# Sums of the last 64 keys as four products of 144 queries for both heads, the two partial sums joined one pair later, and v in one transfer

## The chip, the cores and the metric

The kernel runs on one core of a Trainium2 chip. The metric is the device time of one execution in microseconds; before the change the median of three runs is 551.17 us (551.02 to 552.08). Five engines work side by side, each through its own instructions in order: TensorE (PE, matmuls; its weight loads have a row of their own, PEld), VectorE (DVE), ScalarE (ACT), GpSimd (POOL) and SyncE (SP, which here only issues DMA transfers).

## The reference

Three stages in float32: attention over 4 batches of 8 heads, then a gated layer with a spatial product, then a second gated layer with a short convolution. The change lies in the first.

```python
q_rot, k_rot = (rotate(q), rotate(k))                       # 4 x 8 heads, 576 positions, 64 wide
scores = scale * np.matmul(q_rot, k_rot.transpose(0, 1, 3, 2))
scores = scores - np.max(scores, axis=-1, keepdims=True)
attn = np.exp(scores)
attn = attn / (np.sum(attn, axis=-1, keepdims=True) + 1e-09)
return np.matmul(attn, v)
...
h = gelu(x @ w_in); u, v = halves(h); v_n = layernorm(v) * g_ln
x = x + (u * (w_sg @ v_n + b_sg)) @ w_out                   # then conv gate, w_val, w_out2
```

## The kernel before

Two heads are worked on together: there are 16 **pairs** i = 0 to 15. For a pair, the scores are made transposed (keys on the partitions, 576 queries in two halves of 288) in nine **units**: eight of 128 keys and one half of the queries for both heads (line 663), and a ninth with the last 64 keys of both heads stacked on the 128 partitions (line 671). ACT turns each unit into exponentials, tiles `e0` to `e8` (line 676).

The queries' maxima are found one pair ahead. During the **phase** of pair i (its nine units), TensorE also makes seven score products of pair i+1 with queries on the partitions (line 611 six times, line 621 last), and VectorE reduces them to maxima (lines 614, 629, 623). All these products go through four PSUM slots of two banks. In a phase the slots are used round robin, 0 1 2 3: the first product is one of line 611 in slot 0, and the fifth, a unit of scores, takes slot 0 again, so it needs the first maximum to have been read. The slots come from a small greedy model in the code (`free`, `pe`, `ac`, `dv`).

After its phase a pair is finished: 64 instructions of exponentials by v (line 700; one float32 product is two instructions, and four products run side by side on the four groups of 32 columns of the array), then the **sums** of the exponentials (`sum_unit`, line 735): groups of four products with weights of ones, over pairs of tiles, over the POOL's running sums `ac`, and over `e8`; then the last 64 keys by v (line 710). ACT and DVE copy the result out (`xu`, line 715 on DVE). The sums go by ACT to `ss`, by a DMA to `rc`, and a pair later through a reciprocal (line 747) and a DMA to `r_d` (`sum_end`).

VectorE's work from one phase to the next, here called a **turn**, is in this order: last maximum of pair i+1 (line 623), rotation of pair i+2 (four instructions of line 260), then for pairs 1 to 8 a quarter of a weight's conversion (lines 310 to 316), for pairs 9 to 14 a low part `kl` (line 260), the reciprocal of pair i-1 somewhere among these, the copy `xu` of pair i, and then the first maximum of the next phase. A POOL instruction on one element, `mark` (line 268), holds back the POOL until VectorE has passed its two-input work.

The order on every engine is made by a planner (`Plan.order`): each task has a cost in us, and the planner simulates the engines with these costs; TensorE's order is fixed as written, that of the others follows due times. A changed cost or task can so move others. From about 234 us on the two later stages run (line 843 for most of their products).

Of the kernel before, what the change touches and what calls it, by code (L numbers as in the profile page):

```python
# [170 lines left out]
def mixer_kernel(ctx: ExitStack, tc: tile.TileContext, qk, v, vrem, cs, w_in, g_ln, w_sgT, b_sg,  # L171
# [63 lines left out]
    VM = tiles(att, "vm", 2, [128, 4, 2, 64], F32)  # L235
    VR = tiles(att, "vr", 2, [128, 64], F32)
# [4 lines left out]
    RC = tiles(att, "rc", 2, [128, 9], F32)  # L241
# [5 lines left out]
    ones = att.tile([128, 32], F32, name="ones")  # L247
    ones_b = [att.tile([128, 32], F32, name=f"ones_b{h}") for h in range(2)]
# [27 lines left out]
    def setup():  # L276
# [3 lines left out]
        def consts():  # L280
            nc.gpsimd.memset(one_r.bitcast(F32), 0.0)
            nc.gpsimd.memset(one_b.bitcast(F32), 0.0)
            for h in range(2):
                nc.gpsimd.memset(ones_b[h], 0.0)
            nc.gpsimd.memset(ones, 1.0)
            nc.gpsimd.memset(mhalf, -0.5)
            for t in (*XS, *RB):
                nc.gpsimd.memset(t[:, 0:4], 0.0)
            for h in range(2):
                nc.gpsimd.memset(one_r[64 * h:64 * h + 1, :].bitcast(F32), 1.0)  # L290
                nc.gpsimd.memset(one_b[64 * h:64 * h + 1, 64 * h:64 * h + 64].bitcast(F32), 1.0)
                nc.gpsimd.memset(ones_b[h][64 * h:64 * h + 64], 1.0)
# [355 lines left out]
    ne = [0]  # L648
    EU = {}

    def st_unit(i, u, ps, kps):
# [38 lines left out]
    def pv_unit(i, us):  # L690
# [3 lines left out]
        if us[0] < 8:  # L694
            j = UNITS[us[0]][0]

            def mm():
                for h in range(2):
                    for t in range(4):
                        nc.tensor.matmul(pv[32 * t:32 * t + 32, h, 0:HALF], VM[j2][:, j, h, 32 * (t % 2):32 * (t % 2) + 32],  # L700
# [5 lines left out]
        def mm():  # L706
            for hf in range(2):
                for h in range(2):
                    rows = slice(64 * h, 64 * h + 64)
                    nc.tensor.matmul(pv[64 * hf:64 * hf + 64, h, 0:HALF], VR[j2][rows], e[rows, hf], start=False, stop=True,  # L710
                                     skip_group_check=True)
        add("PE", FP32 + 0.1, mm, [("e", EU[i, 8]), ("vr", j2)], [kp])
# [10 lines left out]
    def sum_unit(i, ps, kps):  # L723

        j2 = i % 2
        src = [(ones, ones, [(E[EU[i, u + hf]], h) for h in range(2) for hf in range(2)], ("e", EU[i, u]),
                ("e", EU[i, u + 1])) for u in (4, 6)[adds(i) // 2 - 1:]]
        src.append((ones, ones, [(AC[hf], h) for h in range(2) for hf in range(2)], ("ac", 0), ("ac", 1)))
# [10 lines left out]
        add("Act", act(HALF), lambda: nc.scalar.activation(ss, ps[:, 0, 0:HALF], AF.Copy, bias=1e-9), [kps], [("ss", 0)])  # L739
# [26 lines left out]
    def attention():  # L766
# [3 lines left out]
        def phase(i, vl):  # L770

            order = "ytyttxtttyttyxTS" if i + 1 < NPAIR else "ttttttttT"
            if not i:
                order = "xtttyttytyttyxTS"
            free = [0.0, 0.0, 0.74 if i else 0.0, 0.0]
            pe, ac, dv = 0.2, 0.0, 0.0
            nt, xs, ys = 0, iter(range(2)), iter(range(2, 6))
            for x, what in enumerate(order):
                ks = range(4) if x < len(order) - 4 else range(3)
                at_once = [k for k in ks if free[k] <= pe]  # L780
                k = max(at_once, key=lambda k: free[k]) if at_once else min(ks, key=lambda k: free[k])
                pe = max(pe, free[k])
                if what in "tT":
                    pe += 4 * PASS if what == "t" else 8 * PASS + 0.24
                    act_at = max(ac, pe + 0.22)
                    ac, free[k] = act_at + 0.55, act_at + 0.75
                    st_unit(i, nt, PS[k], ("ps", k))
                    add_unit(i, nt)
                    nt += 1
# [454 lines left out]
```

## Time and profile before

| | |
|---|---|
| median of 3 runs | 551.17 us (551.02 to 552.08) |
| the profiled execution: its own time | 550.86 us |
| the profiled execution: span, first to last instruction | 549.1 us |
| mean granted TensorE clock | 0.999 |
| busy PE, PEld | 541.2 us, 462.5 us |
| busy DVE, ACT, POOL | 416.6 us, 278.4 us, 245.7 us |
| chain that ended last | PE 97%, DVE 1% |
| line 735 (sums), per instruction | 406 ns, 464 instructions |

The profile's times are microseconds from the span's start. An instruction's duration includes the way through the engine's pipeline, so the next one may start before it ends; what an instruction costs its engine is the step from its start to the next start. Idle time in brackets is that of the engine ahead of the instruction, with what ended it.

### The profile page before, as it was taken

To read this page: it belongs to the slowest core of one execution; us is meant where nothing else is said; L and a number is where in the kernel's file an instruction comes from. 1 tells how busy PE (TensorE), PEld (TensorE's weight loads), DVE (VectorE), ACT (ScalarE), POOL (GpSimd) and SP (SyncE) were. 2 spreads that over 40 slices of the span, in tenths; PEclk is the share of its full clock that TensorE was granted. 3 is DMA by queue.
4 is the path that set the end of the run, shared out by engine and by line. 5 is a ranking of instruction groups with operands and counts; after the bars stand their busy time and mean duration, and the time that the engine had idled before them with its cause. 6 is when DMAs were issued, how large, how long until landed. Compare 5 with 4: busy or idle time off the path is not lost.

```text
span 549.1 us, 12848 instructions
## 1 busy us (share of the span) xinstructions
PE 541.2 (99%) x5104; PEld 462.5 (84%) x5104; DVE 416.6 (76%) x611; ACT 278.4 (51%) x451; POOL 245.7 (45%) x229
## 2 busy tenths in 40 slices
PE   7999999999999999999999999999999999999996
PEld 6877777777777777679989989989999998899985
DVE  7878888888888888878478845663989997659610
ACT  3566767667766667635527136135156443333221
POOL 6545555555555555446886776653610011222000
PEclk9999999999999999999999999999999999999999
DMA  5565656565556673773384752634264212110022
GB/s 193 136 186 154 194 143 189 150 178 175 168 164 161 185 205 95 216 240 93 133 280 134 223 198 74 210 113 144 106 214 130 66 45 78 38 58 1 0 78 96
DMA packets 58028, 77.46 MB, mean 141 GB/s; under 512 B 29392, under 2 KB 34000, under 8 KB 57968
## 3 DMA queue, kind: packets, MB, share of 16 engines
q1 hardware_dynamic: 57664, 76.37, 45.8%
q8 instruction: 40, 0.66, 0.5%
q10 hardware_dynamic: 304, 0.26, 0.1%
q14 instruction: 20, 0.16, 0.1%
HBM read 55.94 MB, written 18.95 MB: 136 GB/s over the span
## 4 chain that ended last, share of the span: by engine, by line
PE 97%; DVE 1%; POOL 0%; ACT 0%; issue 0%; ACTq 0%; POOLq 0%
PE psa L843 55%; PE psa L663 13%; PE psa L700 12%; PE psa L735 5%; PE psa L611 4%; PE psa L671 4%; PE psa L710 2%; PE psa L954 2%; PE psa L756 1%; DVE mx L614 1%; PE psa L621 1%; DVE raw L260 0%; DVE mn L623 0%; POOL mr L295 0%; ACT ob L264 0%
## 5 line engine op out<-in xcount | busy, mean ns | idle before, releaser
L614 DVE TENSOR_REDUCE mx<-psa 128x2 f32<-128x640 f32 (+1 forms) x96 | 88.7, 954 | 21.9 <-PE psa L611 14.6
L676 ACT ACTIVATE e<-psa 128x576 f32<-128x576 f32 x144 | 88.1, 652 | 20.9 <-PE psa L671 10.3
L700 PE MATMUL psa<-e,vm 128*32 128x288 f32 x1024 | 65.4, 408 | 0.0
L700 PEld LDWEIGHTS psa<-e,vm 128*32 128x32 f32 x1024 | 31.6, 110 | 27.8 <-issue 2.6
L261 POOL TENSOR_TENSOR ac<-e,e 128x576 f32<-128x576 f32 x32 | 45.0, 1425 | 8.2 <-ACT e L676 8.2
L843 PE MATMUL psa<-s_h,vn 128*128 128x288 f32 x256 | 46.9, 295 | 0.0
L260 DVE TENSOR_TENSOR raw<-raw,cst 128x1152 f32<-128x1152 f32 (+1 forms) x33 | 41.9, 1271 | 0.3 <-DMA raw<-qk 0.3
L264 ACT CAST qp<-raw 128x512 fp32r<-128x512 f32 x16 | 19.1, 1192 | 43.6 <-DVE raw L260 43.6
L663 PE MATMUL psa<-qh,kh 64*128 64x288 f32 x256 | 39.6, 305 | 0.0
L843 PEld LDWEIGHTS psa<-s_h,vn 128*128 128x128 f32 x256 | 38.3, 188 | 0.0
L663 PE MATMUL psa<-qh,kl 64*128 64x288 f32 x256 | 37.9, 292 | 0.0
L663 PE MATMUL psa<-ql,kh 64*128 64x288 f32 x256 | 37.9, 292 | 0.0
L663 PE MATMUL psa<-mr,one_r 64*128 64x288 f32 x256 | 37.7, 290 | 0.0
L261 POOL TENSOR_TENSOR vs<-vs,u 128x576 f32<-128x576 f32 x16 | 26.7, 1666 | 20.7 <-DVE vs L958 20.7
L611 PE MATMUL psa<-kh,qp 64*128 64x320 f32 (+1 forms) x256 | 32.8, 312 | 0.7 <-ACT kh L264 0.7
L1035 DVE SCALAR_TENSOR_TENSOR gt<-xm,cw,gt 128x576 f32<-128x576 f32 x32 | 28.9, 909 | 1.8 <-ACT gt L1032 1.4
L611 PEld LDWEIGHTS psa<-kh,qp 64*128 64x128 f32 x256 | 21.6, 184 | 8.0 <-ACT ss L739 3.9
L843 PE MATMUL psa<-XL,w_h 128*128 128x288 f32 x128 | 27.4, 296 | 0.0
L843 PE MATMUL psa<-XH,w_h 128*128 128x288 f32 x128 | 27.4, 295 | 0.0
L843 PE MATMUL psa<-XH,w_l 128*128 128x288 f32 x128 | 27.4, 295 | 0.0
L843 PE MATMUL psa<-s_l,vn 128*128 128x288 f32 x128 | 27.2, 294 | 0.0
L261 POOL TENSOR_TENSOR xl<-xs,xh 128x576 fp32r<-128x576 f32 x2 | 4.6, 2322 | 48.8 <-ACT xh L264 48.8
(182 smaller groups left out, 1488.2 us busy)
## 6 DMA issues: line engine op xcount, KB each, us to landing
raw<-qk SPq DMA_DIRECT2D x31, 576.0 KB
xu_d<-xu SPq DMA_DIRECT2D x32, 144.0 KB
rb<-r_d SPq DMA_DIRECT2D x32, 144.0 KB
xs<-xu_d SPq DMA_DIRECT2D x16, 288.0 KB
x_d<-xs SPq DMA_DIRECT2D x16, 288.0 KB
g_d<-vs SPq DMA_DIRECT2D x16, 288.0 KB
vm<-v SPq DMA_DIRECT2D x16, 256.0 KB
wr<-w_in SPq DMA_DIRECT2D x8, 512.0 KB
```

Of the source, the lines that this page charges most:

```text
L260: return add("DVE", dve(n), lambda: nc.vector.tensor_tensor(out_(), a(), b(), op), r, w, after, lock=True)
L261: return add("Pool", pool(n), lambda: nc.gpsimd.tensor_tensor(out_(), a(), b(), op), r, w, after, lock=True)
L264: return add("Act", act(n), lambda: nc.scalar.copy(out_(), in_()), r, w, after)
L611: nc.tensor.matmul(ps[:, h, w * y:w * y + w], QP[j2][rows, c], kh[rows, keys], start=True, stop=True)
L614: add("DVE", MAXIMA[n // 2 > 0][1], lambda: nc.vector.tensor_reduce(out=MX[j2][:, n // 2 > 0, :, chunks[0]:chunks[-1] + 1], in_=ps[:, :, 0 ...
L663: nc.tensor.matmul(ps[:, h, 0:HALF], x[rows, keys] if o < 3 else x[rows], y[rows, cols], start=o == 0, stop=o == 3)
L671: nc.tensor.matmul(ps[:, hf, 0:HALF], x, y[:, cols], start=o == 0, stop=o == 3)
L676: add("Act", 0.62, lambda: nc.scalar.activation(E[n], ps[:, :, 0:HALF], AF.Exp), [kps], [("e", n)])
L700: nc.tensor.matmul(pv[32 * t:32 * t + 32, h, 0:HALF], VM[j2][:, j, h, 32 * (t % 2):32 * (t % 2) + 32], E[EU[i, us[t // 2]]][:, h], start=j ...
L735: nc.tensor.matmul(ps[32 * t:32 * t + 32, 0, 0:HALF], x[t // 2], a[:, y], start=n == 0, stop=n == len(src) - 1, skip_group_check=True)
L843: nc.tensor.matmul(out_(y), lhs(p, k, y), rhs(q, k, y), start=not z, stop=ends and z == len(terms) - 1)
L1035: add("DVE", dve(S) + 0.05, lambda dd=dd, m=m, x2=x2, gt=gt: nc.vector.scalar_tensor_tensor(gt(), x2()[:, m:m + S], cw[:, 5 * dd + m:5 * d ...
```

## The change

- `sum_unit`: the products of `e8` with ones covered 288 queries of one head each (two weights `ones_b`, one for each head's 64 partitions). Now each covers 144 queries and both heads: the weight `ones_b` has ones for head h in columns 16h to 16h+15, and the four products, on the four column groups, take two halves of 288 in two slices of 144. So that a column group can hold both heads, the other sums use two weights `ones0`, `ones1`, with ones in 16 of the 32 columns and zeros in the others. The number of instructions is the same; eight of them per pair are half as long.
- The total of a query then lies in two rows of PSUM. Two DMAs instead of one bring both parts to `rc` (now 128 x 3 x 9), and in `sum_end` a `tensor_reduce` on VectorE adds them ahead of the reciprocal; two DMAs instead of one bring the result to `r_d`.
- `v` and its last 64 keys come in one DMA per pair instead of two.
- Two more memsets in the setup, for the new weights.
- The slots of a phase are written out (`ORDERS`) instead of computed; the numbers are the same as the greedy model gave. The numbers of the `e` tiles are also the same.
- The planner's cost of the sums falls by half a float32 product, and it gets the new tasks.

```diff
+ORDERS = ('xtttyttytyttyxTS', '0123012301230120'), ('ytyttxtttyttyxTS', '0123012301230120'), ('ttttttttT', '012012012')
...
-    RC = tiles(att, "rc", 2, [128, 9], F32)
+    RC = tiles(att, "rc", 2, [128, 3, 9], F32)
...
+            nc.gpsimd.memset(ones_b, 0.0)
             for h in range(2):
-                nc.gpsimd.memset(ones_b[h], 0.0)
-            nc.gpsimd.memset(ones, 1.0)
+                nc.gpsimd.memset(ones[h], 0.0)
+                nc.gpsimd.memset(ones[h][:, 16 * h:16 * h + 16], 1.0)
...
-        def ld(q):
-            q.dma_start(out=VM[j2].rearrange("p c h d -> p (c h d)"), in_=v[i // HP, i % HP])
-            q.dma_start(out=VR[j2], in_=vrem[i // HP, i % HP])
-        dma(290, ld, w=[("vm", j2), ("vr", j2)], after=after, n=2)
+        dma(290, lambda q: q.dma_start(out=VM[j2], in_=v[i // HP, i % HP]), w=[("vm", j2)], after=after)
...
-        src.append((*ones_b, [(E[e], hf) for h in range(2) for hf in range(2)], ("e", e)))
 
         def mm():
             for n, x in enumerate(src):
-                for t, (a, y) in enumerate(x[2]):
-                    nc.tensor.matmul(ps[32 * t:32 * t + 32, 0, 0:HALF], x[t // 2], a[:, y], start=n == 0,
-                                     stop=n == len(src) - 1, skip_group_check=True)
-        add("PE", len(src) * FP32, mm, [*[k for x in src for k in x[3:]], ("consts",)], [kps])
+                for t, (a, h) in enumerate(x[0]):
+                    nc.tensor.matmul(ps[32 * t:32 * t + 32, 0, 0:HALF], ones[h], a[:, h], start=n == 0, stop=False, skip_group_check=True)
+            for t in range(4):
+                cc = slice(144 * (t // 2), 144 * (t // 2) + 144)
+                nc.tensor.matmul(ps[32 * t:32 * t + 32, 0, cc], ones_b, E[e][:, t % 2, cc], start=False, stop=True, skip_group_check=True)
+        add("PE", (len(src) + 0.5) * FP32, mm, [*[k for x in src for k in x[1:]], ("e", e), ("consts",)], [kps])
...
         def rows(q):
-            q.dma_start(out=rc, in_=ss[0:97:32].rearrange("t (p c) -> t p c", c=9))
-        dma(5, rows, [("ss", 0)], [("rc", j2)])
+            for y in range(2):
+                q.dma_start(out=rc[:, y], in_=ss[64 * y:64 * y + 49:16].rearrange("t (p c) -> t p c", c=9))
+        dma(5, rows, [("ss", 0)], [("rc", j2)], n=2)
...
-        add("DVE", 0.25, lambda: nc.vector.reciprocal(rc, rc), w=[("rc", i % 2)], after=after)
-        dma(5, lambda q: q.dma_start(out=r_d[i // HP][i % HP].rearrange("(p c) -> p c", c=9), in_=rc), [("rc", i % 2)], [("r_d", i)])
+        add("DVE", 0.15, lambda: nc.vector.tensor_reduce(out=rc[:, 2], in_=rc[:, 0:2].rearrange("p y c -> p c y"), axis=AX.X, op=ALU.add),
+            w=[("rc", i % 2)], after=after)
+        add("DVE", 0.25, lambda: nc.vector.reciprocal(rc[:, 2], rc[:, 2]), w=[("rc", i % 2)], after=after)
```

How this moves VectorE's work. First the turn after an odd pair (here i = 1), from the last quarter of a conversion (`wf`) to the first maximum (`mx`); `xu` is the copy out of PSUM. Before:

```order
42 L316 SCALAR_TENSOR_TENSOR wf_120<-wr_119,wt_121 128x256
43 L747 RECIPROCAL rc_172<-rc_172 128x9
44 L715 COPY xu_170<-psa 128x288
45 L614 TENSOR_REDUCE mx_151<-psa 128x2 x2
46 L614 TENSOR_REDUCE mx_151<-psa 128x2x2
```

And now:

```order
42 L317 SCALAR_TENSOR_TENSOR wf_120<-wr_119,wt_121 128x256
43 L744 TENSOR_REDUCE rc_170<-rc_170 128x9
44 L746 RECIPROCAL rc_170<-rc_170 128x9
45 L710 COPY xu_168<-psa 128x288
46 L612 TENSOR_REDUCE mx_151<-psa 128x2 x2
```

The joining stands directly ahead of the reciprocal that reads its result, and both ahead of the copy and the maximum. The same holds after pairs 3, 5 and 7, and, behind `kl` instead of `wf`, after pairs 9 to 13.

Then the turn after an even pair (here i = 2), from the last maximum (`mn`, from PSUM) to the copy. Before:

```order
50 L623 TENSOR_REDUCE mn_153<-psa 128x1
51 L747 RECIPROCAL rc_173<-rc_173 128x9
52 L260 TENSOR_TENSOR raw_123<-raw_123,cst 128x1152
53 L260 TENSOR_TENSOR raw_123<-raw_123 128x576
54 L260 TENSOR_TENSOR raw_123<-raw_123,cst 128x1152
55 L260 TENSOR_TENSOR raw_123<-raw_123 128x576
56 L310 TENSOR_SCALAR wt_121<-wt_121 128x256
57 L312 TENSOR_SCALAR wt_121<-wt_121 128x256
58 L314 SCALAR_TENSOR_TENSOR wt_121<-wr_119,wt_121 128x256
59 L316 SCALAR_TENSOR_TENSOR wf_120<-wr_119,wt_121 128x256
60 L715 COPY xu_169<-psa 128x288
```

And now:

```order
51 L621 TENSOR_REDUCE mn_153<-psa 128x1
52 L744 TENSOR_REDUCE rc_171<-rc_171 128x9
53 L260 TENSOR_TENSOR raw_123<-raw_123,cst 128x1152
54 L260 TENSOR_TENSOR raw_123<-raw_123 128x576
55 L260 TENSOR_TENSOR raw_123<-raw_123,cst 128x1152
56 L260 TENSOR_TENSOR raw_123<-raw_123 128x576
57 L311 TENSOR_SCALAR wt_121<-wt_121 128x256
58 L313 TENSOR_SCALAR wt_121<-wt_121 128x256
59 L315 SCALAR_TENSOR_TENSOR wt_121<-wr_119,wt_121 128x256
60 L317 SCALAR_TENSOR_TENSOR wf_120<-wr_119,wt_121 128x256
61 L746 RECIPROCAL rc_171<-rc_171 128x9
```

The joining has taken the reciprocal's place, and the reciprocal stands behind the conversion, just ahead of the copy. The same holds after pairs 4, 6 and 8.

On the POOL, at the program's start, the memsets ahead of those that TensorE waits for. Before, from the first to the one after the weights:

```order
8 L284 MEMSET ones_b_180 128x32
9 L284 MEMSET ones_b_181 128x32
10 L285 MEMSET ones 128x32
11 L286 MEMSET mhalf 128x1
12 L288 MEMSET xs_107 128x4
```

And now:

```order
8 L283 MEMSET ones_b 128x32
9 L285 MEMSET ones_177 128x32
10 L286 MEMSET ones_177 128x16
11 L285 MEMSET ones_178 128x32
12 L286 MEMSET ones_178 128x16
13 L287 MEMSET mhalf 128x1
```

Two memsets are new, and each of the two of 16 columns writes over part of the one just ahead of it.

## Rows read from the trace of the kernel before

**Rows 1.** The page: busy time of the engines, and the chain by engine.
```profile
PE 541.2 (99%) x5104; PEld 462.5 (84%) x5104; DVE 416.6 (76%) x611; ACT 278.4 (51%) x451; POOL 245.7 (45%) x229
...
PE 97%; DVE 1%; POOL 0%; ACT 0%; issue 0%; ACTq 0%; POOLq 0%
```

**Rows 2.** TensorE in order of time, end of pair 3: start, duration, engine, instruction.
```profile
72.06 0.43 PE L735 MATMUL psa<-ac,ones 128*32 128x288 f32 x4
...
72.30 0.67 PE L735 MATMUL psa<-e,ones_b 128*32 128x288 f32 x8
72.90 0.71 PE L710 MATMUL psa<-e,vr 64*64 64x288 f32 x8
73.55 0.41 PE L611 MATMUL psa<-kh,qp 64*128 64x320 f32 x2
```

**Rows 3.** TensorE's weight loads at the fifth product of the next phase.
```profile
74.74 0.19 PEld L663 LDWEIGHTS psa<-mr,one_r 64*128 64x128 f32 x2
74.99 0.19 PEld L663 LDWEIGHTS psa<-qh,kh 64*128 64x128 f32 x2
```

**Rows 4.** VectorE in order of time, the turn after pair 3.
```profile
67.36 0.17 DVE L629 TENSOR_REDUCE mn<-mx 128x8 fp32r<-128x16 f32 x1
67.45 0.75 DVE L623 TENSOR_REDUCE mn<-psa 128x1 fp32r<-128x576 f32 x1
68.12 1.35 DVE L260 TENSOR_TENSOR raw<-raw,cst 128x1152 f32<-128x1152 f32 x1
69.50 0.76 DVE L260 TENSOR_TENSOR raw<-raw 128x576 f32<-128x576 f32 x1
...
73.34 0.42 DVE L316 SCALAR_TENSOR_TENSOR wf<-wr,wt 128x256 int32<-128x256 int32 x1
73.69 0.21 DVE L747 RECIPROCAL rc<-rc 128x9 f32<-128x9 f32 x1
73.81 0.40 DVE L715 COPY xu<-psa 128x288 f32<-128x288 f32 x1
74.12 0.81 DVE L614 TENSOR_REDUCE mx<-psa 128x2 f32<-128x640 f32 x1
```

**Rows 5.** VectorE, the copy after pair 0, then the turn after pair 9.
```profile
32.40 0.46 DVE L715 COPY xu<-psa 128x288 f32<-128x288 f32 x1 [1.47 <-PE psa L710]
...
155.64 0.20 DVE L747 RECIPROCAL rc<-rc 128x9 f32<-128x9 f32 x1
156.02 0.46 DVE L715 COPY xu<-psa 128x288 f32<-128x288 f32 x1 [0.17 <-issue]
```

**Rows 6.** The start: POOL, TensorE and VectorE in order of time.
```profile
1.57 0.12 POOL L292 MEMSET ones_b<- 64x32 f32 x1
1.73 0.20 POOL L290 MEMSET one_r<- 1x128 f32 x1
...
2.77 6.50 PE L756 MATMUL psa<-mr,one_r 128*128 128x512 f32 x16 [2.77 <-POOL mr L295]
...
9.74 3.82 DVE L614 TENSOR_REDUCE mx<-psa 128x4 f32<-128x1024 f32 x4 [0.21 <-PE psa L611]
```

**Rows 7.** From attention to the next stage: VectorE, TensorE, POOL, TensorE.
```profile
232.54 1.58 DVE L260 TENSOR_TENSOR XL<-xs,XH 128x576 fp32r<-128x576 f32 x2
...
234.81 0.73 PE L843 MATMUL psa<-w_h,XH 128*128 128x512 f32 x2
...
249.62 1.30 POOL L261 TENSOR_TENSOR w_l<-wf,w_h 128x512 fp32r<-128x512 f32 x1 [5.25 <-ACT w_h L264]
...
251.47 0.42 PE L843 MATMUL psa<-XH,w_l 128*128 128x288 f32 x2
```

**Rows 8.** VectorE beside the POOL: all of line 629 (min/median/max ns), and single instructions.
```profile
L629 DVE TENSOR_REDUCE mn<-mx x16: 170/170/173, 15.7 to 216.7; 128x8 fp32r<-128x16 f32 x16
...
155.79 0.18 POOL L268 COPY mark<-kl 1x1 f32<-1x1 f32 x1 [5.23 <-DMA raw<-qk]
155.93 0.80 POOL L261 TENSOR_TENSOR s_l<-xs,s_h 128x288 fp32r<-128x288 f32 x1
...
239.22 1.15 DVE L312 TENSOR_SCALAR cwt<-cwt 128x20 int32<-128x20 int32 x1
```

More of the change, by code (lines that the diff above doesn't have):

```diff
@@ L170, in mixer_kernel @@
 @with_exitstack
-def mixer_kernel(ctx: ExitStack, tc: tile.TileContext, qk, v, vrem, cs, w_in, g_ln, w_sgT, b_sg,
+def mixer_kernel(ctx: ExitStack, tc: tile.TileContext, qk, v, cs, w_in, g_ln, w_sgT, b_sg,
                  w_out, w_val, conv_w, w_out2, out):
@@ L246, in mixer_kernel @@
     one_b = att.tile([128, 128], F32R, name="one_b")
-    ones = att.tile([128, 32], F32, name="ones")
-    ones_b = [att.tile([128, 32], F32, name=f"ones_b{h}") for h in range(2)]
+    ones = [att.tile([128, 32], F32, name=f"ones{h}") for h in range(2)]
+    ones_b = att.tile([128, 32], F32, name="ones_b")
     mark = att.tile([128, 1], F32, name="mark")
@@ L646, in s_end @@
         mq[i] = dma(5, rest, [("mn", j2, 1)], [("mr", j2, 2)])
-    ne = [0]
     EU = {}
@@ L699, in mm @@
                     for t in range(4):
-                        nc.tensor.matmul(pv[32 * t:32 * t + 32, h, 0:HALF], VM[j2][:, j, h, 32 * (t % 2):32 * (t % 2) + 32],
+                        nc.tensor.matmul(pv[32 * t:32 * t + 32, h, 0:HALF], VM[j2][:, 128 * j + 64 * h + 32 * (t % 2):128 * j + 64 * h + 32 * (t % 2) + 32],
                                          E[EU[i, us[t // 2]]][:, h], start=j == 0, stop=False, skip_group_check=True)
@@ L709, in mm @@
                     rows = slice(64 * h, 64 * h + 64)
-                    nc.tensor.matmul(pv[64 * hf:64 * hf + 64, h, 0:HALF], VR[j2][rows], e[rows, hf], start=False, stop=True,
+                    nc.tensor.matmul(pv[64 * hf:64 * hf + 64, h, 0:HALF], VM[j2][rows, 512:576], e[rows, hf], start=False, stop=True,
                                      skip_group_check=True)
-        add("PE", FP32 + 0.1, mm, [("e", EU[i, 8]), ("vr", j2)], [kp])
+        add("PE", FP32 + 0.1, mm, [("e", EU[i, 8]), ("vm", j2)], [kp])
         xu = XU[j2]
@@ L725, in sum_unit @@
         j2 = i % 2
-        src = [(ones, ones, [(E[EU[i, u + hf]], h) for h in range(2) for hf in range(2)], ("e", EU[i, u]),
-                ("e", EU[i, u + 1])) for u in (4, 6)[adds(i) // 2 - 1:]]
-        src.append((ones, ones, [(AC[hf], h) for h in range(2) for hf in range(2)], ("ac", 0), ("ac", 1)))
+        src = [([(E[EU[i, u + hf]], h) for h in range(2) for hf in range(2)], ("e", EU[i, u]), ("e", EU[i, u + 1]))
+               for u in (4, 6)[adds(i) // 2 - 1:]]
+        src.append(([(AC[hf], h) for h in range(2) for hf in range(2)], ("ac", 0), ("ac", 1)))
@@ L748, in sum_end, with rows @@
-        dma(5, lambda q: q.dma_start(out=r_d[i // HP][i % HP].rearrange("(p c) -> p c", c=9), in_=rc), [("rc", i % 2)], [("r_d", i)])
+        add("DVE", 0.15, lambda: nc.vector.tensor_reduce(out=rc[:, 2], in_=rc[:, 0:2].rearrange("p y c -> p c y"), axis=AX.X, op=ALU.add),
+            w=[("rc", i % 2)], after=after)
+        add("DVE", 0.25, lambda: nc.vector.reciprocal(rc[:, 2], rc[:, 2]), w=[("rc", i % 2)], after=after)
+        def rows(q):
+            for hf in range(2):
+                q.dma_start(out=r_d[i // HP][i % HP].rearrange("(h x p c) -> x h p c", h=2, x=2, c=9)[hf], in_=rc[64 * hf:64 * hf + 64, 2])
@@ L750, in mixer_kernel @@
+        dma(5, rows, [("rc", i % 2)], [("r_d", i)], n=2)
     mq = {}
@@ L770, in phase @@
         def phase(i, vl):
[L772 to L776, printed above, removed]
-            nt, xs, ys = 0, iter(range(2)), iter(range(2, 6))
[L778 to L782, printed above, removed]
-                if what in "tT":
[L784 to L789, printed above, removed]
-                else:
-                    pe += 2 * PASS if what == "S" else MAXIMA[what == "y"][0]
-                    dve_at = max(dv, pe + 0.29)
-                    dv = dve_at + (0.67 if what == "S" else MAXIMA[what == "y"][1])
-                    free[k] = dv + 0.15
+            nt, xs, ys = 0, iter(range(2)), iter(range(2, 6))
+            for x, (what, k) in enumerate(zip(*ORDERS[(1 if i + 1 < NPAIR else 2) if i else 0])):
+                k = int(k)
+                if what in "tT":
+                    u = 8 if what == "T" else nt
+                    st_unit(i, u, PS[k], ("ps", k))
+                    add_unit(i, u)
+                    nt += what == "t"
+                else:
                     s_unit(i + 1, {"x": xs, "y": ys, "S": iter((8,))}[what].__next__(), PS[k], ("ps", k))
```

14 lines of the change are left out of this document (5 added, 9 removed).

## The prediction

> **What bounds the kernel now.** I read the page first. It says TensorE: busy 541.2 of 549.1 us, 97% of the chain, while VectorE is busy 416.6 [rows 1]. Read so, whatever TensorE is spared comes off the time. But that chain follows busy instructions, and a matmul's record contains its pipeline, so a short wait between two matmuls shows in neither number. So I read second TensorE in order of time over one turn, then its weight loads, then VectorE over the same stretch.
>
> At the fifth product of a phase the weight load starts at 74.99, 0.25 us after the one before it; otherwise these loads follow every 0.13 us [rows 3]. So 0.12 us is lost there, and the reader is to see with what: this product takes slot 0, which VectorE's first maximum is reading; that one runs from 74.12 for 0.81 us, to 74.93 [rows 4], and the load starts 0.06 later.
>
> What does that maximum wait for? In rows 4 each VectorE instruction starts 0.08 before the one ahead has ended, or 0.03 after it where it reads its result (68.12 + 1.35 = 69.47, next start 69.50). From 67.45 to 74.12 there is no gap, and none in the rows left out. Even the copy `xu` at 73.81, which needs TensorE's line 710, starts 0.12 behind the reciprocal, as any instruction there would. So after pairs 1 to 8 VectorE's own chain, from its last maximum to the first one of the next phase, sets when the fifth product starts; all that follows in the phase, to the product whose maximum starts the next turn, hangs on that. Line 735 is not on this loop. TensorE makes its sums beside it and then waits 0.12 us.
>
> Two places differ. After pair 0 there is no conversion and no reciprocal: `xu` waits 1.47 us for line 710 [rows 5], so TensorE is the bound. After pairs 9 to 13 VectorE has less: the reciprocal starts at 155.64 and `xu` only at 156.02, 0.38 later instead of 0.12, idle 0.17 [rows 5]; TensorE bounds it, but by little.
>
> **The change part by part.** The sum is made against the profiled execution's own time, 550.86, which lies 0.31 below the median of the runs, 551.17.
>
> *Shorter products.* The four column groups start together: four instructions in 0.03 us (0.43 against 0.41 for one) every 0.24 us (72.06, 72.30) [rows 2]. A group of eight takes 0.48; at 144 queries I take half of both steps, 0.24 saved per pair. Bounds: 0 if something other than columns sets the step, 0.48 if the group vanished. I take 0.24: both steps are the same for all columns shown.
>
> *After pair 0*: TensorE bounds, so -0.24 is kept. `xu` comes at 32.16 instead of 32.40, and there is nothing before it on VectorE.
>
> *After pairs 1 to 8*: nothing of the 0.24 is kept, TensorE waits 0.36 instead of 0.12. VectorE's chain grows by the joining. Its nearest row is line 629, 16 elements to 8: a step of 0.09 if the next instruction doesn't need it (67.36 to 67.45), and 0.17 + 0.03 = 0.20 if it does [rows 4]. After odd pairs the reciprocal stands right behind and needs it: +0.20, four times. After even pairs the joining takes the reciprocal's place and the reciprocal (0.12, 73.69 to 73.81) moves behind the conversion: it is still paid once, so +0.09, four times. Together 0.80 + 0.36 = +1.16. Bounds: 0.09 in all eight, 0.72; 0.20 in all eight, 1.60.
>
> *After pairs 9 to 13*: joining and reciprocal together put `xu` at 155.64 + 0.20 + 0.12 = 155.96 by VectorE's chain, and TensorE is ready 0.24 earlier than before. So `xu` comes at 155.96 instead of 156.02: -0.06, of which I take 0.05 each, -0.25 for five. The end that excludes more is VectorE's chain; the other end is 0.
>
> *After pair 14 and at pair 15*: no maximum follows; the last phase and the hand-over to line 843 hang on TensorE and ACT alone, so -0.24 twice, -0.48. Cover: the second `XL` ends at 232.54 + 1.58 = 234.12 and line 843 starts at 234.81 [rows 7], 0.48 earlier leaves 0.2. The next to be late is the last low part of `w_in`: the POOL ends it at 250.92, TensorE uses it at 251.47 [rows 7], so 0.07 would be left. Bounds: -0.48 if VectorE's moved conversions and the SP queue leave that chain where it is, up to +0.5 if its load, which has one more DMA of sums ahead of it, comes 1 us later. I take -0.48, as VectorE drops a conversion step from ahead of `XL` and two loads of `r_d` no longer stand behind the reciprocal.
>
> *Start.* Two more memsets; each that overwrites its predecessor must wait for it, a step of 0.16 as from 1.57 to 1.73 [rows 6]. So TensorE's first 16 instructions start up to 0.33 later than 2.77, and VectorE's first maximum waits for what follows them (idle 0.21 at 9.74) [rows 6]. They take 0.41 us each on average (6.50 / 16), and 512 columns at the lower of the two clock levels, 1.2 GHz, are 0.43, so most run there. If the rise to 2.4 GHz comes at the same time as before, half of the 0.33 is given back. Bounds 0 and 0.33; I take +0.20.
>
> *At nothing*: one DMA for `v` instead of two, and two instead of one for `rc` and `r_d`. No TensorE or VectorE instruction waits for them in the rows: `v` is used a phase later, the sums are read a turn later. The covered price is one issue on SP per pair. The slots are the same numbers. ACT's copy of the sums is unchanged.
>
> Sum: 0.20 - 0.24 + 1.16 - 0.25 - 0.48 = **+0.39**: 551.25 for the profiled execution, and with its 0.31 about **551.6** as the median, +0.07%.
>
> **A rule weighed.** The joining and the reciprocal now run nearer to the POOL's work. After pair 9 the reciprocal would start at 155.84, inside `mark` (155.79 to 155.97), and the POOL's next two-input instruction starts at 155.93 [rows 8]. VectorE's instructions of one small shape differ there: line 312, 20 columns, took 1.15 us beside the POOL at 239.22, while all 16 of line 629 took 0.170 to 0.173 [rows 8], most of them inside a POOL instruction. The Trainium skill (SBUF — State Buffer, "SBUF: two separate sides") says that GpSimd and a VectorE instruction that reads two SBUF inputs or runs in a two-port mode lock each other out for a whole instruction, and others don't. By that rule the joining, as line 629, is never held, and the trace agrees (0.173 at most). For the reciprocal no row starts inside a POOL instruction; that is the third rival.
>
> **The rivals.**
> 1. *The page is right*: TensorE keeps all 16 savings, 16 x 0.24 = 3.84, so 547.3. For it: 97% of the chain. Against it: the 0.12 lost at each fifth product with VectorE's maximum ending 0.06 ahead. 8%.
> 2. *Half as many columns are not half the time.* Eight instructions in 0.48 us are 0.06 each; if handing them over is what takes 0.06, all of TensorE's terms vanish: 0.20 + 1.16 = +1.36, 552.5, slower. Against it: four start within 0.03 us and then nothing for 0.21 [rows 2]; a hand-over that set the pace would space them evenly. The Trainium skill (TensorE: Matmul & The Clock Gate, "Wait — 56ns, not 53.3ns?") has such a pace, about 62 ns per matmul in one mode of decoding, and by it the group would stay at 0.5 us. 7%.
> 3. *The reciprocal is held by the POOL*, after pairs 9 to 13, from the point that it starts inside `mark` and the POOL's next instruction (0.80 at 155.93) goes ahead of it: `xu` would start 0.12 after 156.73, at 156.85 instead of 156.02, +0.8 five times, +4.1. With the other terms +4.7: 555.9, slower. For it: line 312's 1.15. Against it: it reads one input of nine columns. 6%.
> 4. *The last weights come late*: the end term is +0.5 instead of -0.48, 552.6. 10%.
>
> **How the numbers follow.** The forecast has 69%. Its terms' bounds give 0 - 0.24 + 0.72 - 0.25 - 0.48 = -0.25 to 0.33 - 0.24 + 1.60 + 0 - 0.48 = +1.2, so 550.9 to 552.4. With half a microsecond below for the spread of runs, and rivals 2 and 4 above, the range is 550.5 to 552.8; rival 1, rival 3 and some ends lie outside, 2 in 10. A measurement of this kernel tells about 0.2% from no change, 1.1 us: faster is below 550.07, slower above 552.27. Faster: rival 1 and 2% of the forecast, 0.10. Slower: rival 2, rival 3, half of rival 4 and a little of the forecast, 0.20. The rest, 0.70, is the same.
>
> **What would show it.** In the new profile, line 735's products of 144 start 0.12 apart instead of 0.24 and line 710 starts 0.24 sooner after line 700's end (else rival 2). The weight load of the fifth product after pairs 1 to 8 waits some 0.4 to 0.5 us, and these turns are longer than before by 0.2 (odd) and 0.09 (even). After pair 0 the turn is 0.24 shorter. `xu` after pair 9 is no longer preceded by idle time. TensorE is late at the start by 0.1 to 0.3. If the fifth product doesn't wait longer, the reading of the loop is wrong, and the time comes out near 547; if VectorE's reciprocal lasts more than 0.25 us after pairs 9 to 13, rival 3 is right.

## The result: 1.2% slower, most of it behind DMA issues that the prediction had put at nothing

| | before | after |
|---|---|---|
| median | 551.17 us (551.02 to 552.94, 5 runs) | 559.23 us (558.51 to 559.97, 5 runs) |
| the profiled execution: its own time | 550.86 us | 558.51 us |
| its span | 549.1 us | 556.7 us |
| after / before, 95% interval | | 1.012 (1.0085 to 1.0156) |

Forecast were 551.6 us and a range of 550.5 to 552.8; the time lies 6.4 us above the range's end.

The span, +7.60, is cut best at the products of line 621 (619 after), one per phase: from the start of one weight load of this line to the next is one turn. (These starts are in TensorE's weight loads in order of time; the sums over turns are worked out from them.) All times in us, as differences from the profiled execution of the kernel before:

| stretch | before | after | difference | predicted |
|---|---|---|---|---|
| to the product in pair 0's phase | 25.08 | 25.21 | +0.13 | +0.20 |
| turn after pair 0 | 13.81 | 13.57 | -0.24 | -0.24 |
| turns after pairs 1 to 8 | 110.31 | 111.87 | +1.55 | +1.16 |
| turns after pairs 9 to 13 | 66.62 | 67.39 | +0.77 | -0.25 |
| from there to the end | 333.28 | 338.67 | +5.39 | -0.48 |

The profile prints its span to a tenth, so the last row is good to 0.1. The sum of the terms was +0.39. Of the 7.2 us that it missed, 0.4 lie in pairs 1 to 8, 1.0 after pairs 9 to 13, and 5.9 behind the last of these products.

### What came as predicted

TensorE after pair 3, in order of time, after the change (to be compared with [rows 2]):

```profile
72.49 0.43 PE L732 MATMUL psa<-e,ones_b 128*32 128x144 f32 x8
72.85 0.72 PE L705 MATMUL psa<-e,vm 64*64 64x288 f32 x8
```

From the first product of `e8` with ones to the product with v it is now 72.85 - 72.49 = 0.36, before 72.90 - 72.30 = 0.60: half as many columns do save 0.24. But in this turn it is not kept. VectorE in the same turn (compare [rows 4]), and the weight loads of the fifth product of the next phase (compare [rows 3]):

```profile
73.87 0.17 DVE L744 TENSOR_REDUCE rc<-rc 128x9 f32<-128x18 f32 x1
74.07 0.21 DVE L746 RECIPROCAL rc<-rc 128x9 f32<-128x9 f32 x1
74.20 0.41 DVE L710 COPY xu<-psa 128x288 f32<-128x288 f32 x1
74.52 0.82 DVE L612 TENSOR_REDUCE mx<-psa 128x2 f32<-128x640 f32 x1
```

```profile
74.91 0.32 PEld L660 LDWEIGHTS psa<-mr,one_r 64*128 64x128 f32 x2
75.39 0.19 PEld L660 LDWEIGHTS psa<-qh,kh 64*128 64x128 f32 x2 [0.17 <-DVE mx L612]
```

The joining costs 74.07 - 73.87 = 0.20, as put, and the first maximum ends at 74.52 + 0.82 = 75.34; the fifth product loads its weights 0.05 later, at 75.39, and now the profile itself names VectorE as what was waited for. In [rows 3] the same step was 0.25 and had no name behind it. Ahead of it, at 74.66, another weight load waits 0.20 for the copy `xu`; the prediction did not foresee that wait, but it is for the same chain on VectorE.

### What did not

Two places. First, the turn after pair 11 (14.02 instead of 13.30): TensorE's products with the maxima `mr` wait for a DMA.

```profile
184.41 0.30 PE L660 MATMUL psa<-ql,kh 64*128 64x288 f32 x2
185.04 0.59 PE L660 MATMUL psa<-mr,one_r 64*128 64x288 f32 x2 [0.33 <-DMA mr<-mn]
```

Second, and much larger, the hand-over to the next stage (compare [rows 7], where the last low part of `w_in` ended 0.55 before its use at 251.47):

```profile
256.02 0.53 PE L832 MATMUL psa<-XH,w_h 128*128 128x288 f32 x2 [3.21 <-ACT w_h L264]
...
257.37 0.85 PE L832 MATMUL psa<-XH,w_l 128*128 128x288 f32 x2 [0.57 <-POOL w_l L261]
258.02 0.68 PE L832 MATMUL psa<-XH,w_h 128*128 128x288 f32 x2
258.50 0.68 PE L832 MATMUL psa<-XL,w_h 128*128 128x288 f32 x2
...
260.85 0.43 PE L832 MATMUL psa<-XH,w_h 128*128 128x288 f32 x2
261.11 0.43 PE L832 MATMUL psa<-XL,w_h 128*128 128x288 f32 x2
```

TensorE stands still for 3.21 and 0.57 us because the last parts of `w_in` are not converted yet. Then it is slow: two products take 0.48 us (258.02 to 258.50) instead of 0.26 (260.85 to 261.11). The view by stretches says why; its columns are the stretch, its length, busy time of PE, PEld, DVE, ACT and POOL, the granted clock, the DMA share and GB/s. After the change:

```profile
255.00:260.00 5.00, 3.41 (x15) 3.19 (x16) 4.89 (x16) 2.08 (x4) 3.63 (x5) 0.74 0.70 183
```

and before:

```profile
255.00:260.00 5.00, 5.00 (x40) 5.00 (x38) 4.45 (x8) 2.51 (x5) 3.56 (x5) 1.00 0.00 0
```

Behind the second wait the granted clock fell, from 2.4 to 1.2 GHz for about 3.5 us (14 products from 257.37 to 260.85 in 3.48 us; at 0.13 each they would take 1.84). So the 5.39 is 3.21 + 0.57 of waiting and some 1.6 of slow clock behind it.

Why were the weights late? First, it is the load that was late, not its conversion. SP's issue of the last load of `w_in`, and ScalarE's and VectorE's first steps on it, after the change:

```profile
245.32 0.38 SPq L324 DMA_DIRECT2D wr<-w_in  x1
251.50 0.66 ACT L321 ACTIVATE wt<-wr 128x512 f32<-128x512 f32 x1 [6.59 <-DMA wr<-w_in]
252.19 0.29 DVE L311 TENSOR_SCALAR wt<-wt 128x256 f32<-128x256 f32 x1 [6.07 <-ACT wt L321]
```

and the first two of them before:

```profile
239.57 0.44 SPq L323 DMA_DIRECT2D wr<-w_in  x1
244.79 0.66 ACT L320 ACTIVATE wt<-wr 128x512 f32<-128x512 f32 x1 [5.04 <-DMA wr<-w_in]
```

Counted from the last product of line 621 (619), ScalarE's step starts 33.47 us later after the change and 28.97 before, 4.50 more: 3.54 of it because the load is issued later (27.29 against 23.75), 0.96 because the transfer takes longer (6.18 against 5.22; why is open). From that step to the end of the last low part it takes 5.82 us, before 6.13.

Second, the issue. The chain of waits before said TensorE for 97% [rows 1]; now it says:

```profile
PE 82%; DVE 7%; DMA 3%; ACT 3%; SPq 2%; issue 1%; POOL 1%; ACTq 0%; POOLq 0%
```

SPq is new in it: SP's queue, which issues the DMAs. SP in order of time after the last product of line 621 (218.03), up to the load of the next-to-last part of `w_in`, where the delay has built up (start, time for the issues merged in the row, line, transfer, how many):

```profile
220.11 0.58 SPq L372 DMA_DIRECT2D bsb<-b_sg  x1
220.74 0.45 SPq L371 DMA_DIRECT2D gsb<-g_ln  x1
221.23 0.44 SPq L374 DMA_DIRECT2D cwr<-conv_w  x1
221.77 1.18 SPq L635 DMA_DIRECT2D mr<-mn  x2
...
226.05 3.64 SPq L843 DMA_DIRECT2D rb<-r_d  x4
229.79 1.00 SPq L839 DMA_DIRECT2D xs<-xu_d  x2
230.89 1.27 SPq L739 DMA_DIRECT2D rc<-ss  x2
232.25 1.12 SPq L750 DMA_DIRECT2D r_d<-rc  x2
233.47 1.30 SPq L714 DMA_DIRECT2D xu_d<-xu  x2
234.82 1.56 SPq L324 DMA_DIRECT2D wr<-w_in  x1
```

and the same before the change, behind its last product of line 621 at 215.82:

```profile
216.92 1.80 SPq L637 DMA_DIRECT2D mr<-mn  x2
...
224.94 0.63 SPq L742 DMA_DIRECT2D rc<-ss  x1
225.67 0.41 SPq L850 DMA_DIRECT2D xs<-xu_d  x1
226.13 0.42 SPq L748 DMA_DIRECT2D r_d<-rc  x1
226.64 1.41 SPq L719 DMA_DIRECT2D xu_d<-xu  x2
228.10 0.59 SPq L323 DMA_DIRECT2D wr<-w_in  x1
```

Both queues run without a pause: 22 issues in 14.71 us after (220.11 to 234.82), 17 in 11.18 before (216.92 to 228.10), about 0.66 us for each. Of the five more, one each is for `rc` and `r_d`; the other three are `bsb`, `gsb` and `cwr`, which the queue before had behind it at 216.92. So SP set the moment of this load before the change as well, and whatever is put ahead of it costs 0.66 apiece. Counted over the trace, 303 issues stood ahead of this load before and 316 after; 316 and 331 ahead of the last one. The next-to-last load is issued 12.28 us after the product of line 621 before, 16.79 after, 4.51 later; of that 3.54 are left at the last load, as the queue before pauses between the two loads (from 228.69 to 230.29, for one) and the changed one hardly does. The change's issues are the cause, as e2_before_dmas below shows: one DMA fewer for `v`, but one more for `rc` and one more for `r_d` per pair.

### The profile page after: what moved, and what is told of

Read it like the earlier page. It is cut to its first block, busy times and chain, and to the rows that moved or that the text cites. A ratio compares the mean times of both kernels' runs of the same rounds, so it can differ in the third digit from the quotient of the medians.

```text
span 556.7 us, 12892 instructions
## 1 busy us (share of the span) xinstructions
PE 543.3 (98%) x5104; PEld 465.3 (84%) x5104; DVE 417.6 (75%) x627; ACT 277.3 (50%) x451; POOL 245.3 (44%) x231
## 4 chain that ended last, share of the span: by engine, by line
PE 82%; DVE 7%; DMA 3%; ACT 3%; SPq 2%; issue 1%; POOL 1%; ACTq 0%; POOLq 0%
PE psa L832 51%; PE psa L660 11%; PE psa L695 7%; DVE raw L260 4%; PE psa L609 3%; PE psa L729 3%; DVE mx L612 2%; PE psa L668 2%; ACT e L671 2%; PE psa L943 2%; PE psa L705 1%; PE psa L759 1%; DMA wr<-w_in 1%; DVE mn L621 1%; SPq L739 1%
## 5 line engine op out<-in xcount | busy, mean ns | idle before, releaser
L660 PE MATMUL psa<-qh,kh 64*128 64x288 f32 x256 | 42.6, 308 | 0.0
L660 PE MATMUL psa<-qh,kl 64*128 64x288 f32 x256 | 40.4, 295 | 0.0
L660 PE MATMUL psa<-mr,one_r 64*128 64x288 f32 x256 | 40.1, 292 | 0.3 <-DMA mr<-mn 0.3
L660 PE MATMUL psa<-ql,kh 64*128 64x288 f32 x256 | 39.5, 291 | 0.0
L660 PEld LDWEIGHTS psa<-qh,kh 64*128 64x128 f32 x256 | 26.3, 184 | 3.4 <-DVE mx L612 1.4
```

What stands on the lines that cost most here:

```text
L660: nc.tensor.matmul(ps[:, h, 0:HALF], x[rows, keys] if o < 3 else x[rows], y[rows, cols], start=o == 0, stop=o == 3)
```

## The experiments

Theory SP: the additional issues of `rc` and `r_d` fill SP's queue from pair 9 on; `mr` and the last two loads of `w_in` come late. Theory VectorE: the joining, and what it moves on VectorE, delays the conversion of the last weights. The differences below are those of the table above: start, after pair 0, after pairs 1 to 8, after pairs 9 to 13, rest.

| kernel | median, runs | ratio to before, 95% | differences by stretch (one profiled execution) |
|---|---|---|---|
| after | 559.23 (5) | 1.012 (1.0085 to 1.0156) | +0.13 -0.24 +1.55 +0.77 +5.39 |
| e2_before_dmas | 556.88 (5) | 1.0105 (1.0086 to 1.0123) | -0.04 +0.03 +1.44 +0.30 +4.28 |
| e4_before_v_one | 550.99 (11) | 0.999 (0.9982 to 0.9999) | -0.25 +0.01 +0.08 -0.04 +0.70 |
| e1_rd_one | 556.40 (12) | 1.0066 (1.0041 to 1.0092) | -0.20 -0.24 +1.17 +0.07 +2.00 |
| e5_weights_act | 556.41 (6) | 1.0096 (1.0068 to 1.0124) | +0.24 -0.24 +1.48 +1.35 +1.97 |
| e3_no_join | 555.60 (10) | 1.0053 (1.0025 to 1.0082) | +0.34 -0.23 +0.41 -0.53 +5.11 |
| e6_cost62 | 554.59 (10) | 1.0048 (1.0026 to 1.0070) | +0.18 -0.25 +1.19 +0.36 +2.72 |
| e7_small_late | 557.84 (6) | 1.0094 (1.0063 to 1.0124) | -0.23 -0.23 +1.55 +2.04 +4.07 |
| e8_pool | 556.49 (6) | 1.0077 (1.0047 to 1.0108) | -0.14 -0.23 -0.04 +3.16 +2.15 |
| e9_relieved | 552.51 (12) | 1.0001 (0.9986 to 1.0016) | -0.21 -0.25 +1.49 -0.24 +0.30 |
| e10_pool8 | 550.91 (12) | 0.9975 (0.9954 to 0.9995) | +0.54 -0.24 -0.58 +0.10 +0.19 |
| b_v_late | 550.94 (12) | 0.9977 (0.9967 to 0.9987) | -0.03 +0.02 +0.03 -0.06 +0.14 |

The ratios are to runs of the kernel before on the same chip (medians there 551.17 to 552.26), so they, not the medians, compare kernels of different rows. The start lies between -0.23 and +0.34 in kernels that do the same there, so a term of 0.2 can't be read from it. The last column, too, is good to 0.1.

**e2_before_dmas: the transfers alone.** The kernel before, with as many DMAs as the changed one: `v` in one (not shown here), `rc` and `r_d` in two each, of 64 partitions.

```diff
-            q.dma_start(out=rc, in_=ss[0:97:32]...)
+            for y in range(2):
+                q.dma_start(out=rc[64 * y:64 * y + 64], in_=ss[64 * y:64 * y + 33:32]...)
...
-        dma(5, lambda q: q.dma_start(out=r_d..., in_=rc), ...)
+            for h in range(2):
+                q.dma_start(out=r_d...[64 * h:64 * h + 64], in_=rc[64 * h:64 * h + 64])
```

> The kernel before, with the DMAs of the changed one alone: v in one, rc in two (64 partitions each), r_d in two. No products of 144, no joining. Theory SP: the last weights come late as in the changed kernel, +4 to +6: 555 to 557. Theory VectorE: nothing waits for these DMAs, 551.2, at most 0.3 away.

Measured 1.0105, 556.88. This settles it against theory VectorE as the cause of the loss: no joining, no shorter product, and yet the waits are there. The view of waits (engine, line, who was waited for: us in total, times, longest):

```profile
PE psa L843 <- ACT w_h L263: 1.7, 1, 1.7
...
PE psa L617 <- DMA qr<-qh: 1.1, 1, 1.1
PE psa L843 <- POOL w_l L260: 0.6, 1, 0.6
```

Besides the last weights, one product of line 617 (621 before) waited 1.1 us for `qr`, the diagonal blocks, in one turn: another small transfer that stood behind the queue (SP issues from 139.09 up to it, at 144.42, without a pause), and nearly all of this kernel's +1.44 in pairs 1 to 8.

**e4_before_v_one: one issue fewer.** The kernel before with the change's single load of `v`.

> The kernel before, with v in one DMA instead of two and nothing else. Theory SP: one issue fewer per pair; the waits on mr after pairs 9 to 13 in the kernel before are small, so 550.7 to 551.2. Theory VectorE: no change, 551.2.

0.999: a little faster at best. The +0.70 at its end is that of one execution, of 551.40 us; in it the last load of `w_in` goes out 24.85 us after the product, later than before (23.75) with 16 issues fewer ahead of it: the planner had put others there. Where SP is not behind, an issue less is worth next to nothing, so the price of an issue can't be read from an average over the kernel.

**e1_rd_one: back to the old number of issues.** The changed kernel with `r_d` stored in the order of the reciprocals; the loads of `rb` and `rr` read it in that order (not shown here).

```diff
-            for hf in range(2):
-                q.dma_start(out=r_d...rearrange("(h x p c) -> x h p c", h=2, x=2, c=9)[hf], in_=rc[64 * hf:64 * hf + 64, 2])
-        dma(5, rows, ...)
+        dma(5, lambda q: q.dma_start(out=r_d...rearrange("(p c) -> p c", c=9), in_=rc[:, 2]), ...)
```

> The changed kernel, but r_d is stored in the order in which the reciprocals lie, in one DMA per pair instead of two; the loads of rb and rr read it from there, two runs of 288 a partition. SP so issues as many DMAs per pair as before the change; VectorE's joining and TensorE's products stay. Theory SP (SP's issues follow each other without pause from pair 9 on, and the 17th issue of a pair pushes the maxima mr and the last two loads of w_in back): turns 9 to 13 lose their +0.8 and the wait for the last weights shrinks from 3.8 us to under 1: 552 to 553. Theory VectorE (the joining delays the conversion of the last weights): no change, 558 to 559.5.

Half a miss. After pairs 9 to 13 the loss is gone as expected (+0.07), and pairs 1 to 8 show the predicted +1.17; but the end is still 2.00 late, and the median is 556.4 rather than 552 to 553. In its trace `mr` of the last pair is issued 2.74 us after the product of line 619, before 1.10: the three loads of `bsb`, `gsb` and `cwr`, needed only much later, stand right ahead of it. So the order in the queue matters too, not the number alone.

**e5_weights_act: the last loads past the queue.** The changed kernel, the last two loads of `w_in` issued by ACT.

```diff
+        if act:
+            return add("Act", 0.55, lambda: nc.scalar.dma_start(out=WR[y]..., in_=src), ...)
...
-        weight_load(place(n), w_in[...], after)
+        weight_load(place(n), w_in[...], after, n >= 6)
```

> The changed kernel, with the loads of the last two parts of w_in (n = 6 and 7) issued by ACT instead of SP, everything else the same. Theory SP: only the end is mended, the wait for the last weights goes (3.8 us and what hangs on it), turns 9 to 13 keep their +0.8: 553.5 to 554.5. Theory VectorE: the conversion of these weights, not their load, is late: 557 to 559.

The end fell from +5.39 to +1.97, as theory SP says; turns 9 to 13 kept their loss and made it larger (+1.35), so the whole is 556.4, not 554. What is left at the end is not the load any more: ScalarE's first step on it starts 29.03 us after the product, before 28.97. But two of VectorE's conversion steps behind it take 1.52 us each (at 249.56 and 251.01) instead of 0.42 and 0.29, beside two sums of the POOL (from 249.38, 3.00 us), and TensorE waits 0.98 and 0.56 us for the weights. So VectorE can make these weights late too, if not by the joining.

**e6_cost62: the planner's price.** One number, what the planner thinks that an issue on SP takes.

```diff
-        return add("SP", 0.53 * n, lambda: fn(nc.sync), r, w, after, lat=1.8 + kb / 200.0, kb=kb)
+        return add("SP", 0.62 * n, lambda: fn(nc.sync), r, w, after, lat=1.8 + kb / 200.0, kb=kb)
```

> The changed kernel with one number changed: the planner's cost of a DMA issue on SP is 0.62 us instead of 0.53, as the trace has it. The same DMAs, in another order. Theory SP, with the order as its lever: the planner now sees that the queue is full and puts the maxima mr and the last w_in ahead of what can wait: 552 to 555. Rival: the number of issues alone decides, whatever their order: 558 to 560.

1.0048 instead of 1.012, with all the DMAs of the changed kernel: more than half of the loss was their order. That the planner at 0.53 saw pauses on SP that the chip did not have, and filled them with loads that could wait, is the likely reading, but not shown.

**e7_small_late: three issues out of the way.** `bsb`, `gsb` and `cwr` behind the last load of `w_in`.

```diff
-    small_weights()
...
     wa_load(7, ())
+    small_weights([len(P.tasks) - 1])
```

> The changed kernel with three loads that are not needed until 265 us (bsb, gsb, cwr) issued behind the last load of w_in instead of ahead of the last two; the conversion of cwr on VectorE moves back with them. Theory SP: three issues of 0.6 us fewer ahead of the load n = 6, the end comes 1.8 us sooner or a little more: 556.5 to 557.5. Rival (VectorE or the POOL, not SP, sets when the last weights are ready): 558.5 or more.

A miss in the whole (557.84), a hit in its place: the load n = 6 is issued 14.40 us after the product of line 619 instead of 16.79, and the end is 1.3 shorter. But in the profiled execution the maxima came later after pairs 11 to 13, and TensorE waited 1.4 us for them. With a full queue the loss moves about.

**e3_no_join: the joining by itself.** As e1_rd_one, without the joining.

```diff
-        add("DVE", 0.15, lambda: nc.vector.tensor_reduce(out=rc[:, 2], in_=rc[:, 0:2]..., op=ALU.add), ...)
-        add("DVE", 0.25, lambda: nc.vector.reciprocal(rc[:, 2], rc[:, 2]), ...)
+        add("DVE", 0.25, lambda: nc.vector.reciprocal(rc[:, 2], rc[:, 0]), ...)
```

> As e1_rd_one (one DMA for r_d), and the joining is left out: the reciprocal is that of the first partial sum alone, so the result is not the reference's. Theory: after pairs 1 to 8 VectorE's chain sets the turn, and the joining alone lengthened it; the turns go back from 13.99 (odd) and 13.87 (even) to 13.79, 1.2 us in all below e1_rd_one, about 555. Rival: the turns are longer for another reason (the transfers of rc, TensorE's later products), and stay at 13.87 to 13.99; 556.4.

The turns after pairs 1 to 8 are 13.78 to 13.81 (apart from one of 14.16), where e1_rd_one has 13.99 to 14.01 after odd and 13.87 to 13.89 after even pairs: the joining is 0.2 and 0.09, as the prediction split it. After pairs 9 to 13 the turns are 13.21 to 13.23 instead of 13.24 to 13.40. Its ratio is 0.0013 below that of e1_rd_one, well inside the intervals, and the end of its profiled execution is as late as that of the changed kernel: what the joining costs is read from the turns, not from the whole.

**e8_pool and e10_pool8: the joining elsewhere.** Both have the reliefs of e1_rd_one and e7_small_late, e10_pool8 that of e6_cost62 too. The joining and the reciprocal go to the POOL, in e8_pool for all pairs, in e10_pool8 for the first eight. The costs below are those of e10_pool8; e8_pool's planner had 0.3 for the sum and 0.6 for the power, a third of what it then took.

```diff
+        add("Pool", 0.25, lambda: nc.gpsimd.tensor_tensor(rc[:, 2], rc[:, 0], rc[:, 1], ALU.add), ...)
+        add("Pool", 1.8, lambda: nc.gpsimd.tensor_tensor(rc[:, 2], rc[:, 2], mone, ALU.pow), ...)
```

> The whole change with its costs taken elsewhere: r_d in one DMA as in e1_rd_one, the three small loads late as in e7_small_late, and the joining and the reciprocal (as a power of -1) on the POOL, off VectorE's chain. By both theories together: turns after pairs 1 to 8 at 13.67 (13.79 less the reciprocal's 0.12; the 0.24 of TensorE allow it), after pair 0 -0.24, after pairs 9 to 13 -0.25, start +0.2, end between 0 and +1.5: 549.3 to 551. If the POOL's small instructions hold VectorE, or come late for the POOL's own work, the turns stay at 13.8 or above and it is 552 or more.

> As e9_relieved, and for the first eight pairs the joining and the reciprocal (as a power of -1) are on the POOL; for the others they stay on VectorE, since the power took 1.79 us there in e8_pool and pushed the POOL's sums back. Turns after pairs 1 to 8 at 13.71 as in e8_pool, 0.7 below the kernel before and 1.9 below e9_relieved: 550 to 551. If the POOL's power pushes its sums back in these turns too, single turns above 14 and 551.5 or more.

In e8_pool the turns after pairs 1 to 7 fell to 13.65 to 13.80, but that after pair 8 was 14.24, and four of the next five 13.83 to 14.57. The POOL after pair 9, in order of time, and VectorE's first rotation of the next turn:

```profile
157.08 1.79 POOL L747 TENSOR_TENSOR rc<-rc,mone 128x9 f32<-128x9 f32 x1
158.85 2.80 POOL L262 TENSOR_TENSOR ac<-e,e 128x576 f32<-128x576 f32 x2
161.62 2.79 POOL L262 TENSOR_TENSOR ac<-ac,e 128x576 f32<-128x576 f32 x2
164.38 0.79 POOL L262 TENSOR_TENSOR s_l<-xs,s_h 128x288 fp32r<-128x288 f32 x1
```

```profile
163.66 2.73 DVE L261 TENSOR_TENSOR raw<-raw,cst 128x1152 f32<-128x1152 f32 x1
```

A power of nine columns takes 1.79 us, and with four sums `ac` per pair the POOL has no such time: its last sum now runs to 164.41 and its next instruction to 165.17, into VectorE's rotation, which starts at 163.66 and takes 2.73 us instead of 1.35 [rows 4]. The Trainium skill (SBUF — State Buffer, "SBUF: two separate sides") says that a VectorE instruction with two SBUF inputs and a GpSimd instruction that reads SBUF lock each other out for a whole instruction; these rows agree with it, the rotation being 1.38 longer. TensorE then waits for `kh`, which ACT makes from the rotated data: 5.9 us in all in this kernel. With the first eight pairs alone on the POOL, e10_pool8 has turns of 13.70 to 13.74 there and is at 0.9975 of the kernel before.

**e9_relieved: the change with SP relieved.** The reliefs of e1, e6 and e7 together, joining on VectorE.

> The changed kernel with all three reliefs of SP together: r_d in one DMA (e1_rd_one), bsb, gsb and cwr behind the last load of w_in (e7_small_late), the planner's cost of an SP issue 0.62 (e6_cost62). Products of 144, two DMAs for rc and the joining on VectorE stay. Theory SP: with SP no longer late the terms of the prediction apply, apart from the one after pairs 9 to 13, which the runs so far put at 0: start +0.15, after pair 0 -0.24, after pairs 1 to 8 +1.2, end -0.4 to +0.8: 551.5 to 553. Rival: the change has a further cost near the end that doesn't come from SP: 554 or more, as in e6_cost62.

552.51, no different from the kernel before (1.0001; the prediction's 551.6 was +0.07%). That the two agree is in part luck, as the stretches differ from their terms: -0.21 for +0.20 at the start, +1.49 for +1.16, +0.30 for -0.48 at the end. Its SP waits for work before the last `mr`, and the next-to-last load of `w_in` goes out at 229.88, 13.27 us after the product of line 619:

```profile
215.84 0.62 SPq L714 DMA_DIRECT2D xu_d<-xu  x1
217.71 1.17 SPq L635 DMA_DIRECT2D mr<-mn  x2
```

The last load is in time here: ScalarE's first step on it starts 28.95 us after the product, before 28.97. TensorE still waits 0.5 us for the last low part, and what is late is its conversion: one step of it on VectorE takes 1.54 us where the other of the same shape takes 0.43. It starts inside a sum of the POOL:

```profile
246.73 1.44 POOL L261 TENSOR_TENSOR xs<-xs,rb 128x576 f32<-128x576 f32 x1 [2.67 <-DMA xs<-xu_d]
246.91 1.54 DVE L315 SCALAR_TENSOR_TENSOR wt<-wr,wt 128x256 int32<-128x256 int32 x1
```

**b_v_late: is it the change at all?** The kernel before with the single load of `v` and the late small loads.

> The kernel before with two reliefs of SP and nothing of the rest: v in one DMA (e4_before_v_one), and bsb, gsb and cwr behind the last load of w_in (e7_small_late). Theory SP: the kernel before waits little for SP, so little is to be had: 550.6 to 551.2. If it is under 550.3, SP set the end of the kernel before as well.

0.9977, the same as e10_pool8. So what e10_pool8 wins over the kernel before is also to be had without products of 144. And beside this kernel, on the same chip, e9_relieved is 1.6 us slower (552.51 against 550.94): with SP relieved in both, the change still loses, most of it after pairs 1 to 8. The products themselves bring 0.24 after pair 0 and, with the POOL's help, 0.07 per turn; more was not shown.

## Why the prediction was wrong, by its own steps

- **Start, +0.20: half shown.** TensorE's first product starts at 3.09 instead of 2.77, 0.32 later, where the two memsets were put at up to 0.33. What is left of that at the product in pair 0's phase can't be told from the scatter of the starts (-0.23 to +0.34).
- **Products take half, 0.24 per pair: right** (0.36 instead of 0.60); rival 2 falls.
- **After pair 0, -0.24: right**, in every kernel with these products.
- **After pairs 1 to 8, +1.16, VectorE's chain sets the fifth product: right** in mechanism and size. e1_rd_one and e6_cost62 give +1.17 and +1.19, e3_no_join shows that it is the joining. Of the +1.55 of the changed kernel 0.4 stand in the turn after pair 5 (14.39), where a maximum started late; what held it is not settled (below). Rival 1, that TensorE keeps all savings, falls with it.
- **After pairs 9 to 13, -0.25:** open. e9_relieved has -0.24, but the three turns of the changed kernel without a wait are as long as before (13.29 to 13.32), and in the others the waits on `mr` and what came with them make +0.77. Rival 3 falls: the reciprocal took 0.21 us there (157.29 below; 0.20 before), though it starts inside the POOL's `mark` (157.24) as feared. (The prediction's "no row starts inside a POOL instruction" misses the last reciprocal before the change, at 241.54, 0.04 before the POOL's end; it took 0.20.)

```profile
157.10 0.16 DVE L744 TENSOR_REDUCE rc<-rc 128x9 f32<-128x18 f32 x1
157.29 0.21 DVE L746 RECIPROCAL rc<-rc 128x9 f32<-128x9 f32 x1
157.47 0.46 DVE L710 COPY xu<-psa 128x288 f32<-128x288 f32 x1
```

  `xu` has no idle time ahead of it, as the prediction said it would not.
- **"At nothing: one DMA for `v` instead of two, and two instead of one for `rc` and `r_d`": the step that failed.** The prediction counted the issue ("the covered price is one issue on SP per pair") and took it as covered because no engine waits for these DMAs. True, and beside the point: an issue delays whatever is queued behind it. The cover was never read. SP's own rows in order of time, which the prediction did not use, would have shown it full: 17 issues without a pause ahead of the next-to-last load of `w_in`, and `mr`, in most turns issued 1.1 us after its product, up to 3.3 us after it in the turns after pairs 10 to 13. What the runs showed in its place: the changed number of DMAs alone, without any other part of the change, makes the end 4.3 us later and the span 6.0 longer (e2_before_dmas).
- **The end, -0.48, with a bound of +0.5:** rival 4 had the right place and mechanism (the last weights come late; 0.07 of cover) and the wrong size. It counted "one more DMA of sums ahead"; there were 13 more ahead of the first of these loads over the kernel and 15 ahead of the last, of which the queue, full since pair 9, had carried 4.5 us along to the first and 3.5 to the last. The slow clock behind the wait, 1.6 us, was in no term. Even with SP relieved the end is +0.30 (e9_relieved), not -0.48: TensorE then waits 0.5 for the last low part, the instruction that the prediction named as next to be late, though for VectorE's conversion and not for its load. That was in no term either.

## What to carry to other kernels

An issue on a DMA queue is work on an engine like any other: before costing it at nothing, read that queue in order of time and look for the pause that is to hold it, and then look at what stands behind it. A kernel whose order comes from a planner is only as good as the planner's prices; one that is 15% too low for the busiest queue cost 4 us here (1.012 against 1.0048). And where a long chain (load, conversion, use) ends just in time, nearly all of a delay is paid (4.5 us late at the first step, 3.8 us of waiting), and the clock can be paid on top.

## What was not expected of the hardware

- An issue on SP takes 0.55 us in the median of the changed kernel, but 9 to 17 in each trace take 1.1 to 2.6: in the changed kernel one of the four `rb` took 1.72 of their 3.64 us, and one `w_in` 1.56. What holds them was not tried.
- The twelve runs of e1_rd_one lie between 552.28 and 559.14 us: those of 556.0 or more show a mean granted clock of 0.992 to 0.997, the others 0.998 or more. In the traces the clock stayed at 1.00 behind the waits of e9_relieved (0.5 us at the hand-over) and of e1_rd_one (1.3 and 0.5) and fell behind those of the changed kernel (3.21 and 0.57), so a wait there can cost about 1.6 us more than its own length.
- In the turn after pair 5 of the changed kernel VectorE's third maximum (line 612) starts at 104.80, 0.4 us after its product was ready, as the POOL passes from one instruction with two inputs (from 103.46, 1.42 us) to the next (from 104.84). The same turn was 14.35 and 14.36 in e5_weights_act and e7_small_late, and 13.99 in e1_rd_one, where the POOL ran a little earlier. Whether the POOL held it is open: a maximum reads one input, from PSUM.
- A power on the POOL (9 columns, 1.79 us) costs more than its sum of 576 columns (1.4).
